# Blank TensorE steps planned up to a share of 0.9 in place of 0.7, with a new set of order keys

## The chip, the cores and the metric

The kernel runs on one core of a Trainium2 chip. The metric is the device time of one execution in microseconds, as the median of several runs. The engines are called PE (TensorE, matrix products), DVE (VectorE), ACT (ScalarE), POOL (GpSimd) and SP (SyncE, which here only issues transfers).

## What is computed

The reference is an attention in which a query may look only at the keys of its own hash bucket, followed by a two-layer feed-forward block:

```python
q_bits = (einsum('bhsd,dk->bhsk', q, proj) > 0)        # 4 batches, 8 heads, 768 rows, 64 wide, 6 bits
mask   = q_bucket[:, :, :, None] == k_bucket[:, :, None, :]
scores = where(mask, scale * q @ k.T, -1e9)
attn   = exp(scores - max) ; attn = attn / (sum + 1e-9)
x      = (attn @ v)                                     # gathered to 3072 rows of 512
h      = x @ w_in                                       # 512 -> 2048
g      = 0.5 * h * (1 + erf(h / sqrt(2)))
out    = g @ w_out                                      # 2048 -> 512
```

## The kernel before

All of the work is written down as steps (`Step`, made by `plan.add`), each with the engine or engines that can do it, a cost per engine, what it needs, the ring of buffers that it takes a slot of, and a key. `Plan.order` then plays the steps through on a model of the engines: whenever an engine is free in the model, it takes the step with the lowest key among those that are ready there. The result is one fixed list, and the program is emitted in that list's order, so that each engine has its instructions in one order that doesn't change at run time. The keys, and for steps that several engines can do a preference per engine, come from the table `PAR`.

**Attention.** A unit is 128 queries of one head against all 768 keys. For batch 0 the first eight heads of the first pass (256 queries, 16 units) and then the second pass (512 queries) run, for the other batches all 768 queries in one pass; 192 units in all. The eight heads of the first pass, five of which are used again in the second, work with float32 scores (36 units): `head_plain` loads a head (L911), moves the keys to the lower partitions (L454 or L450 `K<-Q`), projects it onto the hash vectors on PE (L926, four products), takes signs on ACT (L932) and writes mask rows from the signs on whatever engine is free. There is one buffer for the signs, so the projection of a head waits until the masks of the head before are written. In a unit PE makes the scores (L976 in float32; L978 and L979 in float16 later), DVE their maximum (L982), ACT the exponentials (L996). Then, in batch 0, PE turns the exponentials round through PSUM (L1051, copied out by ACT or DVE as `pt`) and multiplies them by the values in float32 (L1128); in the other batches they are split into a high half (any of three engines) and a low half (DVE, L1011), SP issues a transposing transfer (L1018), and PE multiplies by the values in float16 (L1137). Scores have two PSUM buffers (`s`), everything else of PE shares four (`hp`).

**Weights.** w_in and w_out arrive in 32 transfers, DVE decodes each with three instructions (L742, L747, L752), PE makes sums of squares (L765), and each block is split into a high and a low float16 half.

**Feed-forward.** For each of 12 pieces of 256 rows there are two groups; each has 8 blocks of 12 products with w_in (L1367), their evacuation by ACT (L1377), a gelu by ACT (L1405), a split into halves (high half L450/L454, low half on DVE at L1419), and 8 blocks of 6 products with w_out (L1449). The last product group of a piece is drained by DVE (L1479) and stored. Whatever of this isn't done when the last attention unit ends is left for PE at the end.

**Blank steps.** `add_blank` (L404 to L412) adds 128 optional steps, each with four products of a zero 128x128 tile with itself (L409) into a slot of `hp`. They have the key 5000, behind all others, so the planner puts one in only where PE has nothing else that is ready in the model. It also puts none in where the share of recent time in which the model's PE was active is above `FILL` (0.7): the variable `full` in `order`. A step carries a weight `act` for that share (0.6 for float32 scores, 0.5 for float32 projections, 1 for most), so a PE that does only float32 scores without a pause doesn't count as fully active. Steps that the plan didn't reach when all else was placed are left out. Once in the list a blank step is an instruction like any other: PE runs it at its place, whether or not PE would have had a pause there.

Of the kernel before, what the change touches and what calls it, by code (L numbers as in the profile page):

```python
# [34 lines left out]
GROW = ("p","hl")  # L35

PAR = dict(
    KM=91.05, KM_ACT=-197.05, KM_DVE=73.07, KM_Pool=12.06, RN=-144.89, RT=-17.08, RC_ACT=-242.77, RC_DVE=-47.89,
    XH_ACT=4.7, XH_DVE=-82.19, XH_Pool=87.66, XL_DVE=89.94, XL_Pool=357.43, VB=-258.79, GU_DVE=128.11,
    GU_Pool=-25.12, SH_DVE=118.63, SH_ACT=328.9, SH_Pool=79.99, SF_DVE=143.39, SF_ACT=-210.56, SF_Pool=-126.49,  # L40
    SU=-27.59, NM_DVE=371.98, NM_ACT=81.69, NM_Pool=10.86, NM_SP=-49.3, NL_DVE=-98.16, NL_Pool=534.95, NK_DVE=206,
    NK_ACT=268.55, NK_Pool=141.99, Z=140.46, VS0=156.74, H0=141.06, HL=-168.99, VS=-5.57, G2=140.72, HQ=274.94,
    VQ=-118.77, in0=-452.28, out0=234.8, in1=178.74, out1=35.31, in2=-733.22, out2=42.81, in3=-257.05, out3=-39.12,
    H1=85.11, H2=-180.28, H3=-76.25, H4=-254.49, H5=599.36, H6=267.16, H7=-91.77, MEV=211.52, MGE=10.33, MSP=148.58,
    V0=130.06, QK0=757.86, QK1=394.91, QK2=-27.6, MX0=5.05, MX1=-340.43, MX2=-112.33, EX0=-363.39, EX1=-245.52,
    EX2=174.69, NR0=190.13, NR1=-108.68, NR2=-84.17, HI0=-114.82, HI1=-178.05, HI2=438.46, LO0=-267.63, LO1=-47.95,
    LO2=-1120.34, PV0=-759.1, PV1=34.43, PV2=-112.01, TR0=102.85, TR1=-188.58, TR2=162.62, V1=405.09, V2=-110.24,
    Sin0=389.65, Sin1=4.89, Sin2=-162.86, Sin3=184.08, Sout0=112.78, Sout1=-94.3, Sout2=-76.09, Sout3=124.51,
    Lin=297.95, Pin=102.99, Qin=672.15, Cin=28.97, Min=-82.56, Lout=25.44, Pout=-325.05, Qout=524.38, Cout=-497.62,
    Mout=109.33, G0=17.44, G1=-32.16, G3=-43.19, G4=148.57, G5=171.52, G6=-434.49, G7=115.01, DUP0=113.75,  # L50
    DUP1=88.45, DUP2=1354.21, LOW0=225.26, LOW1=166.21, LOW2=29.11, PRJ0=120.95, PRJ1=279.7, PRJ2=-425.18,
    MSK0=-273.6, MSK1=129.08, MSK2=-126.48, DI_ACT=4.6, DI_DVE=81.25, DI_Pool=367.94, WS_ACT=-138.04, WS_DVE=-169.9,
    WS_Pool=156.82, WH_ACT=60.55, WH_DVE=42.49, WH_Pool=-4.63, WL_ACT=-275.05, WL_DVE=200.58, WL_Pool=-447.71,
    VH_ACT=500.86, VH_DVE=-763.86, VH_Pool=-164.87, RND_ACT=178.09, RND_DVE=126.86, RND_Pool=168.39, HI_ACT=65.35,
    HI_DVE=-0.25, HI_Pool=-348.7, EV_ACT=-270.89, EV_DVE=-778.22, EV_Pool=-113.05, GH_ACT=-94.28, GH_DVE=72.85,
    GH_Pool=-34.78, NS0=-43.2, NS1=520.91, NS2=-67.43,
)
FULL = 65504.0
BIG = 2.0**34
# [18 lines left out]
class Plan:  # L78
# [17 lines left out]
    QUEUE = 2.0  # L96
    PORT = 0.1
    WINDOW = 3.413
    FILL = 0.7
    FALLS = 0.45  # L100

    def __init__(self, rings):
# [3 lines left out]
    def add(self, engine, cost, emit, key, needs=(), takes=None, table=None, port=False, act=1.0, spare=False):  # L106
        s = Step(len(self.steps), engine, cost, emit, key, needs, takes, table, port, act, spare)
        self.steps.append(s)
        return s
# [12 lines left out]
    def order(self):  # L122
# [34 lines left out]
        while events and count < total:  # L157
# [25 lines left out]
            for engine, pool in ready.items():  # L183
# [3 lines left out]
                if engine == "PE":  # L187
                    w = int(now / self.WINDOW)
                    share = busy.get(w, 0.0) / self.WINDOW
                    share += busy.get(w - 1, 0.0) / self.WINDOW * (w + 1 - now / self.WINDOW)  # L190
                    full = share > self.FILL
                for s in pool:
# [75 lines left out]
def tile_bucket_attention_moe(  # L268
# [193 lines left out]
    def affine_on(name, n, pointer=False, cuts=0.0):  # L462

        more = 0.11 if name == "RND" else 0.0
        return {
            e: (affine_cost(e, n, pointer) + more + cuts * (e == "Pool"), PAR[f"{name}_{e}"])
            for e in ("ACT", "DVE", "Pool")
        }
# [35 lines left out]
    def set_up():  # L504
# [36 lines left out]

        key = PAR["SU"]
        a = add("Pool", 1.4, sums, key, [])
# [63 lines left out]
    def head(b, h, i, key, clear, cl):  # L607
# [90 lines left out]
        for half in range(2):  # L698
            for k, dst in enumerate((0, 1)):
                box = []  # L700

                def mask(half=half, k=k, dst=dst, box=box):
# [6 lines left out]
                on = {  # L709
                    "DVE": (0.18, PAR["NK_DVE"]), "ACT": (0.53, PAR["NK_ACT"]), "Pool": (0.56, PAR["NK_Pool"])  # L710
                }
# [160 lines left out]
    def values_whole(b, pr, key):  # L872
        def load():
            nc.sync.dma_start(out=whole_of(raw, pr), in_=v[b, :, words(pr)].rearrange("(c p) d -> p c d", p=P))

        raw = add("SP", 1.43, load, key - PAR["VQ"], takes="vhl")
        return raw, raw
# [6 lines left out]
    def values_halves(b, pr, key, scaled):  # L884
# [13 lines left out]

        raw = add("SP", 1.43, load, key - PAR["VQ"], takes="vraw")
        hi = add(affine_on("VH", S, True), 0, high, key, [raw, scaled], takes="vhl", port=True)  # L900
# [4 lines left out]
    def head_plain(b, h, i, key, clear, cl):  # L905
# [10 lines left out]
        loaded = add("SP", 0.85, load, key - PAR["HQ"], clear)  # L916
        mv = add(affine_on("KM", S), 0, move, key + PAR["KM"], [loaded], port=True)
        space = add("none", 0, lambda: None, key, [loaded], takes="sign")
# [20 lines left out]
        for half in range(2):  # L939
            for k, x in enumerate(both_of):  # L940
                box = []

                def mask(half=half, k=k, x=x, box=box):
# [6 lines left out]
                on = {  # L950
                    "DVE": (0.27, PAR["NK_DVE"]), "ACT": (0.53, PAR["NK_ACT"]), "Pool": (0.56, PAR["NK_Pool"])
                }
# [588 lines left out]
```

## Time and profile before

| | us |
|---|---|
| median of 3 runs | 893.41 (890.1 to 893.73) |
| the profiled execution | 894.34 |
| its span, first to last instruction | 892.5 |
| PE busy | 862.8 (97%) |
| DVE busy | 668.4 (75%) |
| ACT busy | 616.0 (69%) |
| POOL busy | 445.8 (50%) |
| blank products on PE (220) | 18.2 |
| start of the last attention score product | 708.97 |

The busy share is a mean over three stages: the start (loads, weights, float32 attention), a middle in which attention and feed-forward run side by side, and an end from 709 us in which only feed-forward is left. The columns of a stretch by engine say more than the mean.

### The profile page before, as it was taken

Reading aid. Unit: us, or ns where it says so; the run is one execution under the profiler, and the core shown is the slowest. Engines: PE = TensorE matmul, PEld = TensorE weight load, DVE = VectorE, ACT = ScalarE, POOL = GpSimd, SP = SyncE. Lnnn points to the kernel's source line nnn. Section 1 sums busy time; section 2 is a strip of 40 time slices with the busy share of each in tenths; the row PEclk is TensorE's granted clock in tenths of the full one; section 3 lists DMA queues with packets and bytes.
Section 4 is the critical chain, followed back from the end, with each engine's and each line's share of the span. In section 5 each row is a group of like instructions: output and inputs, shape, how many; then the busy total and the mean of one; then the engine's idle time right before and its main releaser. Section 6 shows DMA issues by size and latency. Waiting matters only on the chain. (4 is left out here: it accounts for less than half of the span.)

```text
span 892.5 us, 18301 instructions
## 1 busy us (share of the span) xinstructions
PE 862.8 (97%) x6953; PEld 577.6 (65%) x6953; DVE 668.4 (75%) x1356; ACT 616.0 (69%) x1058; POOL 445.8 (50%) x560
## 2 busy tenths in 40 slices
PE   7999999999999999999999999999999999999998
PEld 4566666676667757656657657667657667576663
DVE  5999798998899898988889889878897841212122
ACT  4767868799898778896979887897864823232221
POOL 2437948487666658666756675674752500000000
PEclk9999999999999999999999999999999999999999
DMA  9753261415789899797788988868787540000000
GB/s 311 238 175 105 76 182 38 145 46 107 168 168 172 160 219 186 133 170 160 133 154 198 166 154 151 146 126 146 134 136 125 113 95 1 24 1 24 1 25 24
DMA packets 282424, 112.34 MB, mean 126 GB/s; under 512 B 228704, under 2 KB 269920, under 8 KB 282336
## 3 DMA queue, kind: packets, MB, share of 16 engines
q1 hardware_dynamic: 282032, 111.18, 58.6%
q8 instruction: 54, 0.88, 0.4%
q14 instruction: 34, 0.28, 0.1%
q10 hardware_dynamic: 304, 0.00, 0.0%
HBM read 43.13 MB, written 6.29 MB: 55 GB/s over the span
## 5 line engine op out<-in xcount | busy, mean ns | idle before, releaser
L1367 PE MATMUL hp<-x,Win 128*128 128x256 f16 x2304 | 265.9, 272 | 0.3 <-DVE x L1162 0.2
L1449 PE MATMUL hp<-Wout,g 128*128 128x512 f16 x1152 | 262.6, 379 | 0.0
L1367 PEld LDWEIGHTS <-Win 128*128 128x128 f16 x2304 | 224.1, 98 | 37.5 <-issue 2.4
L1449 PEld LDWEIGHTS <-g 128*128 128x128 f16 x1152 | 110.9, 98 | 124.5 <-issue 2.8
L982 DVE TENSOR_REDUCE rows<-s 128x1 f32<-128x768 f32 x192 | 180.1, 947 | 8.9 <-PE s L976 4.0
L996 ACT ACTIVATE p<-s,rows 128x768 f32<-128x768 f32 x143 | 141.3, 989 | 12.1 <-POOL rows L454 3.8
L1377 ACT ACTIVATE h<-hp,ffs 128x512 f32<-128x512 f32 x96 | 65.5, 683 | 99.6 <-PE hp L1367 99.1
L978 PE MATMUL s<-Q 88*128 88x384 f16 x304 | 99.5, 327 | 7.3 <-ACT p L996 4.1
L979 PE MATMUL s<-K 128*128 128x384 f16 x304 | 99.2, 326 | 0.0
L454 DVE TENSOR_SCALAR g<-h,ffs 128x512 f16<-128x512 f32 x28 | 14.2, 509 | 110.6 <-ACT h L1405 79.4
L987 POOL TENSOR_SCALAR rows<-rows,hs 128x1 f32<-128x1 f32 x84 | 58.9, 702 | 44.0 <-DVE rows L982 39.4
L1137 PE MATMUL hp<-pt,vhl 128*64 128x256 f16 x1296 | 77.2, 274 | 2.6 <-DMA pt<-wraw 1.0
L1011 DVE SCALAR_TENSOR_TENSOR hl<-p,rows,hl 128x768 f16<-128x768 f32 x68 | 70.8, 1043 | 11.5 <-POOL hl L454 8.1
L1419 DVE SCALAR_TENSOR_TENSOR g<-h,ffs,g 128x512 f16<-128x512 f32 x96 | 75.7, 801 | 3.9 <-POOL g L454 1.1
L1137 PEld LDWEIGHTS <-vhl 128*64 128x64 f16 x1296 | 69.2, 110 | 12.5 <-issue 10.7
L476 POOL TENSOR_TENSOR K<-raw,Q 64x768 f16<-64x768 f32 x37 | 63.6, 1718 | 3.1
L454 POOL TENSOR_SCALAR rows<-rows 128x1 f32<-128x1 f32 x95 | 38.3, 403 | 36.2 <-ACT p L996 16.9
L996 ACT ACTIVATE wraw<-s,rows 128x768 f32<-128x768 f32 x49 | 48.4, 987 | 9.9 <-POOL rows L454 6.8
L979 PEld LDWEIGHTS <-K 128*128 128x128 f16 x304 | 29.8, 98 | 28.5 <-issue 12.6
L454 POOL TENSOR_SCALAR raw<-raw,hs 64x768 f32<-64x768 f32 x39 | 43.8, 1122 | 5.4 <-ACT Q L450 1.9
L978 PEld LDWEIGHTS <-Q 88*128 88x128 f16 x304 | 29.7, 98 | 25.8 <-issue 8.5
L1405 ACT ACTIVATE h<-h 128x2048 f32<-128x2048 f32 x24 | 45.9, 1911 | 0.4
(176 smaller groups left out, 1322.4 us busy)
## 6 DMA issues: line engine op xcount, KB each, us to landing
raw<-qk SPq DMA_DIRECT2D x27, 384.0 KB, 3.9
vraw<-v SPq DMA_DIRECT2D x24, 384.0 KB, 4.0
wraw<-w_in SPq DMA_DIRECT2D x16, 512.0 KB, 5.3
wraw<-w_out SPq DMA_DIRECT2D x16, 512.0 KB, 3.9
out<-o SPq DMA_DIRECT2D x11, 512.0 KB, 3.1
K<-Q SPq DMA_DIRECT2D x32, 96.0 KB, 2.3
Q<-qk SPq DMA_DIRECT2D x6, 384.0 KB, 8.0
Q<-Q SPq DMA_DIRECT2D x19, 96.0 KB, 2.3
```

The lines of the kernel that those rows point to most:

```text
L454: on.tensor_scalar(out=o, in0=x, scalar1=scale, scalar2=bias, op0=ALU.mult, op1=ALU.add)
L476: on.tensor_tensor(out=o, in0=x, in1=y, op=ALU.subtract)
L978: nc.tensor.matmul(to, aq[kk, qs], ak[kk, n], start=True, stop=False)
L979: nc.tensor.matmul(to, bq[:, qs], bk[:, n], start=False, stop=True)
L982: nc.vector.tensor_reduce(out=nm, in_=both(sp), axis=AX.XY, op=ALU.max, negate=True)
L996: nc.scalar.activation(out=buf(ex).rearrange("p (b k) -> p b k", b=2), in_=both(sp), func=AF.Exp, scale=sc, bias=nb, accum_out=ssum,)
L1011: nc.vector.scalar_tensor_tensor(out=buf(hi)[:, 1], in0=buf(ex), scalar=r, in1=buf(hi)[:, 0], op0=ALU.mult, op1=ALU.subtract,)
L1137: nc.tensor.matmul(pv[j * D : (j + 1) * D], buf(vh)[:, tv, kt, j * D : (j + 1) * D], buf(holds[j][0])[:, tp * KT + kt, :nt], start=kt == 0 ...
L1367: nc.tensor.matmul(buf(pair[0])[:, j * ch[1] : (j + 1) * ch[1]], win_hl[:, f0 // WB1, tw, pr, f0 % WB1 : f0 % WB1 + P], x[:, tx, pr, : ch[1]],
L1377: nc.scalar.activation(out=values_of()[:, 2 * fp : 2 * fp + 2, :nt], in_=buf(pair[0])[:, : 2 * nt].rearrange("p (j k) -> p j k", j=2), fun ...
L1419: nc.vector.scalar_tensor_tensor(out=gt[:, 1, s2, :nt], in0=h[:, s2, :nt], scalar=sg, in1=gt[:, 0, s2, :nt], op0=ALU.mult, op1=ALU.subtract,)
L1449: nc.tensor.matmul(buf(banks[u]).rearrange("p (c f) -> p c f", c=NWB), gt[:, tg, f, u * P : (u + 1) * P], wout_hl[:, :, tw, ft], start=ft ...
```

## The change

One number of the planner and all of the numbers of `PAR` differ; no other line does.

```diff
 PAR = dict(
-    KM=91.05, KM_ACT=-197.05, KM_DVE=73.07, KM_Pool=12.06, RN=-144.89, RT=-17.08, RC_ACT=-242.77, RC_DVE=-47.89,
+    KM=338.56, KM_ACT=93.78, KM_DVE=-125.94, KM_Pool=-40.06, RN=20.65, RT=-108.24, RC_ACT=-170.72, RC_DVE=19.05,
...
-    FILL = 0.7
+    FILL = 0.9
```

The steps are the same, except for the number of blank products: 220 before, 244 now. What differs is where each step stands, and which engine does the steps that several can do.

The first place is on PE near the start, at the third score unit. In the names `Q_90` and `K_91` are a head's queries and keys, `p` the exponentials, `hash` the hash vectors, `diag` and `sums` small tiles, and the numbers are buffers. Before, from the scores of that unit on:

```order
L976 MATMUL s_61<-K_91,Q_90 128x384 x2
L976 MATMUL s_62<-K_91,Q_90 128x384 x2
L1051 MATMUL hp_63<-ident_131,p_67 128x128 x3
L1051 MATMUL hp_64<-ident_131,p_67 128x128 x3
L1051 MATMUL hp_65<-ident_131,p_68 128x128 x3
L1051 MATMUL hp_66<-ident_131,p_68 128x128 x3
L926 MATMUL hp_63<-Q_116,hash_140 32x384 x4
L409 LDWEIGHTS blank
L409 MATMUL hp_64<-blank 128x128
```

Now, at the same unit:

```order
L976 MATMUL s_61<-K_91,Q_90 128x384 x2
L1051 MATMUL hp_65<-ident_131,p_67 128x128 x3
L1051 MATMUL hp_63<-ident_131,p_67 128x128 x3
L926 MATMUL hp_66<-Q_94,hash_140 32x384 x4
L976 MATMUL s_62<-K_91,Q_90 128x384 x2
L491 LDWEIGHTS ones
L491 MATMUL hp_65<-diag_87,ones 128x128
L1051 MATMUL hp_63<-ident_131,p_68 128x128 x3
L1051 MATMUL hp_66<-ident_131,p_68 128x128 x3
L926 MATMUL hp_65<-Q_116,hash_140 32x384 x4
L976 MATMUL s_61<-K_93,Q_92 128x384 x2
L976 MATMUL s_62<-K_93,Q_92 128x384 x2
```

Before, 12 blank products follow this piece, and 80 stand between the third and the 22nd unit; now none stands there. Ahead of the third unit there are now 148 in place of 112: 24, 24, 40, 32 and 28 in a row, where there were 24, 16, 4, 32, 8 and 28.

The second place is on SP at its very start. Before, the loads of weights (`wraw<-w_in`) stand between those of the heads (`<-qk`):

```order
L911 DMA x_110<-qk 128x768
L735 DMA wraw_82<-w_in 128x2x512
L735 DMA wraw_83<-w_in 128x2x512
L911 DMA Q_114<-qk 128x768
L911 DMA Q_88<-qk 128x768
L617 DMA raw_77<-qk 128x768
L735 DMA wraw_84<-w_in 128x2x512
L911 DMA Q_90<-qk 128x768
```

Now five heads come first, and `Q_88`, of which the first scores are made, is third; its projection on PE is the third one in both orders:

```order
L911 DMA Q_114<-qk 128x768
L911 DMA Q_90<-qk 128x768
L911 DMA Q_88<-qk 128x768
L911 DMA x_110<-qk 128x768
L911 DMA Q_92<-qk 128x768
L735 DMA wraw_82<-w_in 128x2x512
L735 DMA wraw_83<-w_in 128x2x512
L735 DMA wraw_84<-w_in 128x2x512
```

The third place is on PE late in the second pass, after the last projection of a head and before the first products with w_out. Before, 20 blank products stand in a row there, behind the projection (L685):

```order
L685 MATMUL hp_66<-K_95,hash_136 32x384
L409 LDWEIGHTS blank
L409 MATMUL hp_63<-blank 128x128
...
L1051 MATMUL hp_64<-ident_131,p_67 128x128 x3
L1051 MATMUL hp_63<-ident_131,p_67 128x128 x3
L978 LDWEIGHTS Q_92
L978 MATMUL s_62<-Q_92 128x384
```

Now 28 stand ahead of the two small products L577 (which serve a head's scale) and 32 behind them, and then come scores:

```order
L409 MATMUL hp_64<-blank 128x128
L577 LDWEIGHTS twin
L577 MATMUL hp_65<-tops,twin 128x1
...
L409 LDWEIGHTS blank
L409 MATMUL hp_63<-blank 128x128
...
L978 LDWEIGHTS Q_90
L978 MATMUL s_62<-Q_90 128x384
```

Between the 22nd unit and the first product with w_out there are 88 blank products (28 before), and ahead of that first product stand 192 products with w_in (168 before) and 19 float16 units (18 before). Behind the last score of all, 696 products with w_in, 432 with w_out and 108 with values remain (720, 438 and 108 before). Eight blank products now stand after the very last product.

## Rows read from the trace of the kernel before

**Rows 1.** The page's busy times: microseconds, share of the span and instructions of each engine.

```profile
PE 862.8 (97%) x6953; PEld 577.6 (65%) x6953; DVE 668.4 (75%) x1356; ACT 616.0 (69%) x1058; POOL 445.8 (50%) x560
```

**Rows 2.** Busy time of each engine by stretch (from:to, length, then PE, weight loads, DVE, ACT, POOL with instructions in brackets, the granted clock of PE, the share of the DMA engines, GB/s).

```profile
0.00:26.50 26.50, 19.87 (x182) 12.25 (x182) 16.36 (x43) 13.83 (x21) 7.55 (x25) 1.00 0.93 319
26.50:100.00 73.50, 68.65 (x502) 44.48 (x499) 67.75 (x144) 51.76 (x100) 42.77 (x68) 1.00 0.49 152
100.00:209.70 109.70, 104.99 (x923) 76.39 (x921) 97.84 (x230) 89.64 (x170) 73.32 (x107) 1.00 0.33 92
209.70:709.10 499.40, 489.62 (x4090) 325.72 (x4089) 440.65 (x868) 410.36 (x707) 318.27 (x357) 1.00 0.83 156
709.10:892.50 183.40, 179.68 (x1268) 118.79 (x1265) 45.75 (x74) 50.36 (x62) 3.94 (x5) 1.00 0.09 25
200.00:250.00 50.00, 49.43 (x389) 32.95 (x388) 43.59 (x83) 45.11 (x80) 34.79 (x39) 1.00 0.72 137
200.00:425.00 225.00, 219.80 (x1826) 145.44 (x1825) 201.29 (x398) 188.91 (x336) 153.22 (x168) 1.00 0.84 163
```

**Rows 3.** PE in order of time up to the third score unit: start, duration, engine, line, tiles, shapes, count, and in brackets the idle time before it and who ended it.

```profile
0.98 2.74 PE L409 MATMUL hp<-blank 128*128 128x128 bf16 x24 [0.98 <-DVE hash L392]
6.58 1.50 PE L926 MATMUL hp<-x,hash 64*32 64x384 f32 x8 [2.87 <-DVE hash L399]
9.85 0.59 PE L409 MATMUL hp<-blank 128*128 128x128 bf16 x4
11.09 1.44 PE L409 MATMUL hp<-blank 128*128 128x128 bf16 x12 [0.65 <-DVE both_offs L535]
12.46 1.51 PE L926 MATMUL hp<-Q,hash 64*32 64x384 f32 x8
15.68 1.50 PE L926 MATMUL hp<-Q,hash 64*32 64x384 f32 x8
17.76 1.72 PE L409 MATMUL hp<-blank 128*128 128x128 bf16 x28 [0.25 <-DVE hs L580]
19.61 2.82 PE L976 MATMUL s<-K,Q 76*128 76x384 f32 x8
22.36 0.85 PE L926 MATMUL hp<-Q,hash 64*32 64x384 f32 x8
23.59 0.62 PE L765 MATMUL hp<-Win 128*128 128x128 bf16 x8
26.49 2.85 PE L976 MATMUL s<-K,Q 76*128 76x384 f32 x8
```

**Rows 4.** PE in order of time between the third score unit and the last: the two largest pauses of the float32 stretch, the blank product behind the 22nd unit, the 20 blank products in a row and what follows them, the first products with w_out, and the last product of the last score.

```profile
34.82 0.85 PE L926 MATMUL hp<-Q,hash 64*32 64x384 f32 x8 [0.90 <-DVE pt L454]
46.06 1.56 PE L976 MATMUL s<-K,Q 76*128 76x384 f32 x4 [0.97 <-ACT p L996]
...
99.98 0.39 PE L409 MATMUL hp<-blank 128*128 128x128 bf16 x4
...
191.40 1.29 PE L409 MATMUL hp<-blank 128*128 128x128 bf16 x20
193.49 0.88 PE L1051 MATMUL hp<-ident,p 128*128 128x128 f32 x6 [0.80 <-ACT p L996]
...
209.74 1.46 PE L1449 MATMUL hp<-Wout,g 128*128 128x512 f16 x6
...
708.97 0.33 PE L979 MATMUL s<-K 128*128 128x384 f16 x1
```

**Rows 5.** The costliest groups, DVE: line, engine, operation, tiles and shapes, count, then busy microseconds, mean nanoseconds of one, and idle time before them with who ended it.

```profile
L982 DVE TENSOR_REDUCE rows<-s 128x1 f32<-128x768 f32 x192 | 180.1, 947 | 8.9 <-PE s L976 4.0 <-PE s L979 3.6 <-POOL Wout L476 0.3
L651 DVE SCALAR_TENSOR_TENSOR K<-raw,hs,Q 64x768 f16<-64x768 f32 x15 | 18.4, 1225 | 0.4
L454 DVE TENSOR_SCALAR pt<-hp 128x384 f32<-128x384 f32 x34 | 18.2, 547 | 0.9 <-PE hp L1051 0.7 <-PE hp L1128 0.2
L454 DVE TENSOR_SCALAR o<-Wout,tiny 128x1024 f32<-128x1024 f32 x1 | 0.7, 742 | 0.0
```

**Rows 6.** The same view for ACT.

```profile
L450 ACT ACTIVATE hl<-p,rows 128x768 f16<-128x768 f32 x32 | 29.8, 931 | 17.7 <-DMA pt<-hl 8.8 <-DVE rows L987 3.8 <-DVE rows L1005 2.7
L450 ACT ACTIVATE Q<-Q 64x768 f16<-64x768 f16 x7 | 5.9, 842 | 0.1
```

**Rows 7.** Three pieces of the chain that ended last (start, duration, engine, tile, line, count): products with w_in, with w_out and with values, in a stretch where PE doesn't pause.

```profile
584.81 3.93 PE hp L1367 x36
579.59 2.59 PE hp L1449 x12
588.74 2.09 PE hp L1137 x36
```

**Rows 8.** Waits of PE: its tile and line, whom it waited for, microseconds in total, times, longest.

```profile
PE s L978 <- ACT p L996: 4.1, 9, 1.1
PE s L978 <- ACT wraw L996: 2.7, 4, 1.2
PE hp L1137 <- DMA pt<-wraw: 1.0, 2, 0.8
```

**Rows 9.** The end of the run, all engines in order of time.

```profile
884.36 5.53 SPq L1492 DMA_DIRECT2D out<-o  x2
888.82 0.69 DVE L1479 TENSOR_TENSOR o<-hp,ffs 128x512 f32<-128x512 f32 x1 [4.49 <-PE hp L1449]
```

More of the change, by code (lines that the diff above doesn't have):

```diff
@@ L37 @@
 PAR = dict(
-    KM=91.05, KM_ACT=-197.05, KM_DVE=73.07, KM_Pool=12.06, RN=-144.89, RT=-17.08, RC_ACT=-242.77, RC_DVE=-47.89,
[L39 to L56, printed above, removed]
+    KM=338.56, KM_ACT=93.78, KM_DVE=-125.94, KM_Pool=-40.06, RN=20.65, RT=-108.24, RC_ACT=-170.72, RC_DVE=19.05,
@@ new lines @@
+    XH_ACT=210.16, XH_DVE=7.74, XH_Pool=90.78, XL_DVE=-38.28, XL_Pool=158.1, VB=-151.09, GU_DVE=-336.98,
+    GU_Pool=82.95, SH_DVE=-5.82, SH_ACT=-334.92, SH_Pool=-49.18, SF_DVE=21.85, SF_ACT=-104.94, SF_Pool=195.36,
+    SU=-83.27, NM_DVE=86, NM_ACT=-377.53, NM_Pool=-30.66, NM_SP=96.75, NL_DVE=-136.18, NL_Pool=196.74,
+    NK_DVE=-120.63, NK_ACT=-102.29, NK_Pool=10.06, Z=128.09, VS0=-88.2, H0=-48.93, HL=-59.64, VS=129.22, G2=3.26,
+    HQ=295.77, VQ=110.09, in0=79.2, out0=106.24, in1=141.19, out1=168.42, in2=136.87, out2=-115.55, in3=3.35,
@@ new lines @@
+    out3=68.94, H1=191.2, H2=-99.08, H3=-118.34, H4=-332.48, H5=-80.76, H6=254.37, H7=-127.62, MEV=276.73,
+    MGE=-178.16, MSP=66.8, V0=-72.8, QK0=-93.51, QK1=-108.37, QK2=108.6, MX0=-450, MX1=-150.62, MX2=115.85,
+    EX0=-64.03, EX1=137.4, EX2=25.14, NR0=-8.44, NR1=-67.14, NR2=1035.93, HI0=78.66, HI1=110.34, HI2=154.08,
+    LO0=102.73, LO1=-341.19, LO2=-125.71, PV0=190.15, PV1=69.77, PV2=62.11, TR0=227.29, TR1=61.09, TR2=92.8,
+    V1=-72.28, V2=-97.32, Sin0=-126.57, Sin1=-110.63, Sin2=-73.46, Sin3=233.87, Sout0=-26.39, Sout1=-410.31,
@@ new lines @@
+    Sout2=-240.13, Sout3=-125.09, Lin=254.46, Pin=800.99, Qin=-200.36, Cin=121.44, Min=208.69, Lout=-586.01,
+    Pout=-56.05, Qout=-674.79, Cout=322.69, Mout=105.44, G0=-90.72, G1=43.02, G3=94.77, G4=-158.67, G5=-135.69,
+    G6=471.19, G7=52.78, DUP0=-52.55, DUP1=146.67, DUP2=382.24, LOW0=196.35, LOW1=-139.71, LOW2=61.45, PRJ0=158.56,
+    PRJ1=-57.69, PRJ2=85.39, MSK0=129.53, MSK1=30.9, MSK2=-29.16, DI_ACT=-204.87, DI_DVE=-62.27, DI_Pool=-86.29,
+    WS_ACT=-98.19, WS_DVE=-8.9, WS_Pool=-0.46, WH_ACT=133.09, WH_DVE=-86.05, WH_Pool=77.47, WL_ACT=140.41,
@@ L57 @@
+    WL_DVE=123.78, WL_Pool=92.94, VH_ACT=288.88, VH_DVE=110.93, VH_Pool=54.59, RND_ACT=153.06, RND_DVE=-61.11,
+    RND_Pool=-75.2, HI_ACT=-187.83, HI_DVE=119.13, HI_Pool=-61.07, EV_ACT=-109.55, EV_DVE=178.44, EV_Pool=-39.2,
+    GH_ACT=-77.39, GH_DVE=20.88, GH_Pool=170.2, NS0=38.42, NS1=6.74, NS2=221.4,
 )
```

## The prediction

> **What bounds the kernel now.** I read the busy times first, then the same by stretch, then each engine in order of time, and last the waits. PE is busy 862.8 of 892.5 us, far above DVE with 668.4 [rows 1], and the stretches say where the rest is [rows 2]. From 709.1 us PE is alone: 179.68 busy of 183.40, and what is missing there is the last drain and store [rows 9]. From 209.7 to 709.1 it pauses for 499.40 - 489.62 = 9.8 us, mostly until exponentials have freed a score buffer [rows 8]. Before 209.7 it pauses for 6.6, 4.9 and 4.7 us in the three stretches, and there also run the 220 blank products: the kernel's slack lies at the start. With PE's work fixed, the time is that work, plus the blanks, plus the pauses, so a new order can give back at most some 45 us, and each change of order is worth what it does to blanks and pauses.
>
> The start is bound differently from the rest. Between 26.5 and 100 us DVE is busy 67.75 of 73.50 us, nearly as long as PE with 68.65, which includes the blanks [rows 2]. PE pauses there for a copy by DVE or for exponentials [rows 4], and both engines have to be fed for that stretch to shorten.
>
> **The price of a blank.** 24 in a row took 2.74 us at 0.98 us, 0.114 each; 28 in a row took 1.72 us at 17.76, 0.061 each [rows 3]. The projections show the same step: 1.50 at 6.58, 12.46 and 15.68 us, 0.85 at 22.36. So PE runs at its lower level (1.2 GHz) up to about 17 us and at the upper (2.4 GHz) from there, though the clock column reads 1.00 in all stretches [rows 2]. A blank in a real pause costs nothing; one ahead of work that was ready costs its time.
>
> **Part by part, in order of time.** FILL decides only how many blanks stand in the list; nearly all else that moves is moved by the keys.
>
> (a) *Up to the third score unit: +1.0 us.* 36 more blanks stand there. Before, the second projection starts at 12.46, the third at 15.68, the first score at 19.61, the third unit at 26.49 [rows 3]. Now 20 blanks follow from 11.09 (a slot had to come free there) at 0.114: 13.4. The projection takes 1.5: 14.9. Of the next 40 blanks some 20 run slowly, until 17.1, and 20 at 0.061: 18.3. There the third projection starts, 2.6 us late. From it to the first score were 19.61 - 15.68 = 3.9 us, for signs and masks; less the 0.65 that the projection takes less at full clock, the first score comes at 21.6 if the 32 blanks (2.0 us) fit between. Then two units (1.4 each), two projections (0.8 each) and 28 blanks (1.7) stand ahead of the third unit, which comes at about 27.8, 1.3 late. One projection more and one set of squares (0.6) fewer are done by then, which leaves +1.0. The bounds are 0 (DVE, which has other work there, decides) and +2.4. The loads of five heads ahead of the weights bring the scores no earlier, since the buffer for signs lets one head through at a time.
>
> (b) *Third to 22nd unit: -3.0 us.* PE's work there is the same but for one set of squares; 80 blanks are gone, 80 x 0.061 = 4.9 us, beside 4.9 us of pauses. Were PE the only bound, this would give nearly 9.8. But DVE has the same 67.75 us of work there and only 73.50 - 67.75 = 5.8 us to spare [rows 2], so 5.8 is the most. I take half of it, as DVE has to wait for others here and there too. Bounds -5.8 and 0: the pauses can stay where the blanks were.
>
> (c) *22nd unit to the first product with w_out: +1.0 us.* 60 more blanks stand here, 60 x 0.061 = 3.7 us. Before, the 20 in a row took 1.29 us and the exponentials came another 0.80 later [rows 4], so at least there PE really had nothing to do. On the other side DVE gets less to do before its first low half of g: three score maxima (0.947 each) and five copies of pt (0.547) fewer, three 128x1024 pieces of weights (0.742) fewer; three low halves of heads (1.225) and two subtractions of 128x1024 weights more [rows 5]. The trace has none of those on DVE; by the maximum over 768 and by the 768-wide low halves it is 0.9 to 1.7, and I take 1.3. That makes -2.8 - 2.7 - 2.2 + 3.7 + 2.6 = -1.4 us, and small steps as much again. So from all extra blanks (+3.7) to a gain of 1.0: I take +1.0. 24 products with w_in and a score unit are done here that stood later; that moves work, and PE's total stays.
>
> (d) *The middle: 0.* At the last score 24 products with w_in (36 took 3.93 us, so 2.6) and 6 with w_out (12 took 2.59, so 1.3) less are left for the end [rows 7]: 3.9 us less behind that point. It is a gain only if the last score comes at the same time, so if the 3.9 us fit into PE's 9.8 us of pauses; if PE has no more pauses than it had, the last score comes 3.9 later and nothing changes. Added steps: ACT gets nine more high halves of exponentials (0.931) and five more copies (0.842) over the run [rows 6], and small ones, some 14 us in all; POOL gets 29 us less, DVE about 4 more. ACT has 499.4 - 410.4 = 89 us to spare and DVE 59 [rows 2]. I take 0, between -4 and +6.
>
> (e) *The end: 0.* The eight last blanks start when the last product is through, beside the drain (0.69) and the store, which end the run at 892.5 [rows 9].
>
> Sum: +1.0 - 3.0 + 1.0 = -1.0 us on the profiled 894.34, that is 893.3. The median before is 893.41, 0.9 lower, so I predict 892.4.
>
> **A rule against the change.** From 17 us on, PE shows the upper level in all rows, with pauses up to 0.97 us among them [rows 4]. More blanks have no clock to win there, and fewer could lose one. The Trainium skill ("TensorE: Matmul & The Clock Gate", Part 1, The HAM clock gate) says that the lower level is the default and comes back after an idle stretch of PE. The trace agrees for the level at the start and shows no return. By that rule the 80 blanks that go in (b) were a guard.
>
> **The rivals.**
>
> *Faster: the start packs.* In (b) DVE gets its whole 5.8 us, and in (c) the blanks fall into pauses and DVE's relief counts (-1.0). With (a) at +1.0 that is -5.8; with 1 us from the middle -6.8, so 886.6. For it: PE's order from the third to the 22nd unit has no filler left, so whatever DVE releases PE can use. Against it: DVE at 67.75 of 73.50 us is hardly ever free there. Chance 0.32.
>
> *Slower: ACT comes late in the middle.* ACT makes the exponentials on which PE already waits [rows 8]. From 200 to 425 us it is busy 188.91 of 225.00 us, and its densest 50 us are 45.11 [rows 2]. By the 112th unit the new order has given it the larger part of its 14 us more, which would bring that stretch to about 200, or 89%, close to the 90% of the densest piece. If half of the 14 can't be hidden, PE waits 7 us more: 892.4 + 7 = 899.4. It decides from 5.5 us on. For it: the waits on exponentials are the largest of PE's. Against it: part of that work comes earlier rather than in addition, and POOL, which is relieved by 29 us, also feeds the exponentials. Chance 0.18.
>
> *Slower: the clock falls in (b)*, where the scores run in float32 without fillers. At the lower level 10 us of PE's work cost 10 more, so about 902. Against it: PE has 60 us of work there in at most 73, and pauses were never over 1 us after 17 us. Chance 0.05.
>
> *The change does nothing*, since the clock was full and PE's sum is fixed: then 893.4, inside my forecast.
>
> **How the numbers follow.** About 0.5%, 4.5 us, is what a measurement of this kernel can tell from no change: 888.9 and below is faster, 897.9 and above slower. The forecast of 892.4 with the case of no effect has 0.45; faster 0.32; slower 0.18 + 0.05 = 0.23. The likeliest case alone reaches from 889 to 897. For 8 in 10 the range must take in most of the faster and of the first slower case: with (b) at -5.8, (c) at -1, (d) at -3 and (a) at +1 the time is 884.6; with (d) at +6 and (c) at +3 it is 900.4, and the slower cases lie at 899 and 902. I give 884 to 901.
>
> **What would show it.** (a): third score unit at 27 to 28 us in place of 26.49. (b): what follows the 22nd unit comes at 97 to 99 us in place of 99.98 [rows 4], DVE over 93% busy between. (c): the 60 blanks run without a pause behind them if they cost, and with one if they were free; the first product with w_out between 209 and 213 us (209.74 before [rows 4]). (d): the last score at 707 to 713 us in place of 709 [rows 4], and 175.5 to 176 us from it to the end of PE's work; PE's waits on exponentials of 6 to 8 us. ACT's share above 90% between 200 and 425 us, with those waits above 12 us, would speak for the slower rival; a projection or score at double length after 17 us for the clock. I am wrong altogether if PE's pauses in the middle go far from 9.8 us, since no term above prices a shift of that order there.

## The result, and the profile after

The changed kernel takes 897.41 us (median of 6 runs, 895.13 to 899.64) beside 892.82 for the kernel before in the same comparison: a ratio of 1.0053, 95% interval 1.0038 to 1.0069. I had forecast 892.4, no change. The profiled execution is one of 898.22 us with a span of 896.4, so 3.9 more than before.

The page's busy times [rows 1]:

```profile
PE 866.5 (97%) x6977; PEld 580.7 (65%) x6977; DVE 675.8 (75%) x1364; ACT 629.8 (70%) x1081; POOL 416.5 (46%) x525
```

Busy time by stretch, cut at the marks of the prediction (third score unit, blanks behind the 22nd, first product with w_out, last score), and two pieces of the third stretch; columns as in [rows 2]:

```profile
0.00:28.35 28.35, 21.43 (x212) 14.90 (x212) 17.54 (x43) 12.36 (x20) 6.47 (x23) 1.00 0.95 326
28.35:94.35 66.00, 62.09 (x425) 39.62 (x423) 63.20 (x130) 52.07 (x110) 31.16 (x52) 1.00 0.49 154
94.35:216.60 122.25, 116.46 (x1020) 83.88 (x1018) 107.04 (x245) 100.74 (x186) 76.45 (x112) 0.97 0.35 93
216.60:716.70 500.10, 490.12 (x4085) 325.83 (x4082) 442.91 (x877) 415.10 (x708) 300.31 (x337) 1.00 0.79 153
716.70:896.40 179.70, 176.37 (x1247) 116.52 (x1244) 45.13 (x73) 49.53 (x60) 2.15 (x3) 1.00 0.10 24
100.00:125.00 25.00, 22.41 (x197) 14.21 (x197) 22.67 (x46) 15.59 (x36) 8.43 (x13) 0.93 0.68 187
125.00:150.00 25.00, 23.73 (x179) 17.21 (x181) 19.42 (x50) 21.78 (x37) 18.58 (x28) 0.93 0.23 65
```

The clock column is new: 0.97 in the third stretch, 0.93 in two of its pieces, where the kernel before has 1.00 in every row [rows 2]. The second stretch is 7.5 us shorter than before (73.49), the third 12.5 longer (109.72), the middle 0.8 longer and the end 3.8 shorter.

PE in order of time [rows 3, 4]: the start, then the places where the clock falls, the blanks near 185 us, and the marks:

```profile
11.11 2.29 PE L409 MATMUL hp<-blank 128*128 128x128 bf16 x20 [0.80 <-DVE both_offs L535]
13.33 1.50 PE L926 MATMUL hp<-Q,hash 64*32 64x384 f32 x8
18.24 0.85 PE L926 MATMUL hp<-Q,hash 64*32 64x384 f32 x8
22.15 1.56 PE L976 MATMUL s<-K,Q 76*128 76x384 f32 x4
28.35 1.51 PE L976 MATMUL s<-K,Q 76*128 76x384 f32 x4
...
94.35 1.72 PE L409 MATMUL hp<-blank 128*128 128x128 bf16 x28
...
101.30 1.56 PE L976 MATMUL s<-K,Q 76*128 76x384 f32 x4
105.23 1.44 PE L1051 MATMUL hp<-ident,p 128*128 128x128 f32 x6 [2.37 <-DVE hl L454]
106.59 3.72 PE L1128 MATMUL hp<-pt,vhl 128*64 128x256 f32 x20
...
129.53 1.82 PE L1367 MATMUL hp<-x,Win 128*128 128x256 f16 x9 [0.78 <-DVE hs L580]
...
185.25 0.61 PE L409 MATMUL hp<-blank 128*128 128x128 bf16 x8
186.57 1.28 PE L409 MATMUL hp<-blank 128*128 128x128 bf16 x20 [0.72 <-DVE pt L454]
187.90 1.95 PE L409 MATMUL hp<-blank 128*128 128x128 bf16 x32
...
216.62 1.47 PE L1449 MATMUL hp<-Wout,g 128*128 128x512 f16 x6
...
716.73 0.33 PE L979 MATMUL s<-K 128*128 128x384 f16 x1
```

Behind the scores at 101.30 PE waits 2.37 us for a copy by DVE. What follows runs at the lower level (1.2 GHz): 20 products of L1128 take 3.72 us; 24 take 2.81 at the upper level (experiments below). Six products of L1051 take 1.44 us where they took 0.82 at 99.24. A second such piece follows at 129.53, where 9 products with w_in take 1.82 us (12 take 1.47 in e1, last section); PE's pauses just before it are 0.78 us at most.

DVE just there, in order of time, and POOL beside it:

```profile
100.74 0.89 DVE L742 TENSOR_SCALAR Wout<-wraw 128x512 int32<-128x512 int32 x1 [0.97 <-DMA wraw<-w_out]
101.55 2.12 DVE L752 SCALAR_TENSOR_TENSOR Wout<-wraw,Wout 128x512 int32<-128x512 int32 x1
103.70 1.01 DVE L651 SCALAR_TENSOR_TENSOR K<-raw,hs,Q 64x768 f16<-64x768 f32 x1
104.75 0.42 DVE L454 TENSOR_SCALAR hl<-hp 128x256 f32<-128x256 f32 x1
...
101.43 1.69 POOL L476 TENSOR_TENSOR K<-raw,Q 64x768 f16<-64x768 f32 x1
```

The copy of hl, which frees PE's slot, stands in DVE's order behind two steps of decoding w_out. DVE waits 0.97 us for their transfer, and the second takes 2.12 us in place of the usual 0.68.

PE's waits for exponentials [rows 8] are no longer than they were:

```profile
PE s L978 <- ACT p L996: 4.6, 13, 0.8
PE hp L1051 <- DVE hl L454: 2.4, 1, 2.4
PE s L978 <- ACT wraw L996: 0.8, 2, 0.6
```

### The profile page after: what moved, and what is told of

It reads as the page before. It is cut to its first block, busy times and chain, and to the rows that moved or that the text cites. A ratio compares the mean times of both kernels' runs of the same rounds, so it can differ in the third digit from the quotient of the medians.

```text
span 896.4 us, 18331 instructions
## 1 busy us (share of the span) xinstructions
PE 866.5 (97%) x6977; PEld 580.7 (65%) x6977; DVE 675.8 (75%) x1364; ACT 629.8 (70%) x1081; POOL 416.5 (46%) x525
## 5 line engine op out<-in xcount | busy, mean ns | idle before, releaser
L996 ACT ACTIVATE p<-s,rows 128x768 f32<-128x768 f32 x140 | 138.0, 987 | 29.4 <-POOL rows L454 21.2
L978 PE MATMUL s<-Q 88*128 88x384 f16 x304 | 99.3, 327 | 6.4 <-ACT p L996 4.6
L454 DVE TENSOR_SCALAR g<-h,ffs 128x512 f16<-128x512 f32 x34 | 17.9, 529 | 108.4 <-ACT h L1405 77.8
L987 POOL TENSOR_SCALAR rows<-rows,hs 128x1 f32<-128x1 f32 x68 | 50.7, 746 | 63.1 <-DVE rows L982 43.4
L476 POOL TENSOR_TENSOR K<-raw,Q 64x768 f16<-64x768 f32 x38 | 66.2, 1741 | 3.2
L996 ACT ACTIVATE wraw<-s,rows 128x768 f32<-128x768 f32 x52 | 51.3, 986 | 10.0 <-POOL rows L454 6.9
L454 POOL TENSOR_SCALAR hl<-p,rows 128x768 f16<-128x768 f32 x32 | 34.8, 1089 | 40.4 <-DMA pt<-hl 28.1
```

Of the source, the lines that this page charges most:

```text
L454: on.tensor_scalar(out=o, in0=x, scalar1=scale, scalar2=bias, op0=ALU.mult, op1=ALU.add)
L476: on.tensor_tensor(out=o, in0=x, in1=y, op=ALU.subtract)
L978: nc.tensor.matmul(to, aq[kk, qs], ak[kk, n], start=True, stop=False)
L996: nc.scalar.activation(out=buf(ex).rearrange("p (b k) -> p b k", b=2), in_=both(sp), func=AF.Exp, scale=sc, bias=nb, accum_out=ssum,)
```

## The experiments

The theory: the loss stands between the 22nd unit and the first product with w_out; the new order makes pauses of PE there behind which the clock falls, at places where it has no blanks. The rivals: the blanks themselves cost their time; a hole near 185 us, where ACT is away for the first gelu, got longer; DVE has too much to do there. The runs go by the first part of their labels (e1 to e16), each with the median of the kernel before on the same chip in brackets where it is first told, and with its ratio to it. Runs of different chips are set beside each other by their distance from their own kernel before; for the changed kernel that is 4.6 us.

**What the blanks are worth.** Four kernels leave blanks out, by their place among the planned ones; one lets the old keys plan with 0.9. The 60 near 185 us out of the changed kernel:

```diff
         for s in steps:
+            n_blank += s.spare
+            if s.spare and 44 < n_blank <= 59:
+                continue
             s.emit()
```

> The changed kernel without the 60 blank products that stand in a row late in the second pass (185 to 190 us in its trace); every other instruction in the same order. If the order is what costs (PE has nothing to run there, because ACT is loading tables and making the first gelu and so makes no exponentials), the blanks are free and the time stays at the 897.4 us of the changed kernel within 1 us, or rises by about 1.7 us if the clock now falls in the hole. If the blanks cost their own time, it falls by 60 x 0.061 = 3.7 us to 893.7.

897.05 us [893.42], 1.0043 (1.0027 to 1.0059): no gain. The scores behind that place start 5.38 us after the last product ahead of it without the blanks (180.99 to 186.37) and 5.39 us after it with them (184.42 to 189.81), so the 3.7 us that I had charged for them were not on the path. In its profile the clock falls in that hole instead. All 96 behind the third unit out (`n_blank > 37`):

> The changed kernel without all 96 blank products behind the third score unit (28 at 94 us, 60 at 185 us, 8 at the end). If the order costs: 897 to 901 us, with one or two falls of the clock more than the two of the changed kernel, about 1.7 us each. If the blanks cost: 88 x 0.061 = 5.4 us less, 892.0.

896.71 us, 1.0051 (1.0030 to 1.0072): nothing either; the clock is at the lower level from 104.6 us for 3.4 us and from 186.5 for 6.8. The same in the kernel before (`n_blank > 28`, 108 out):

> The kernel before without its 108 blank products behind the third score unit, order otherwise the same. If those blanks hold the clock up, the clock falls here once to three times between 30 and 210 us, where the kernel before has no fall, and the time rises by about 1.7 us a fall to 894.5 to 898. If the blanks cost their own time and hold nothing, 108 x 0.061 = 6.6 us less, 886. If they are free and hold nothing, 892.8.

899.72 us, 1.0077 (1.0058 to 1.0096). Busy time by stretch in that run, second stretch and two of its pieces:

```profile
26.49:99.98 73.49, 64.85 (x385) 39.53 (x382) 63.37 (x132) 47.03 (x91) 36.24 (x58) 0.88 0.44 140
50.00:75.00 25.00, 22.42 (x127) 14.74 (x128) 21.55 (x48) 13.39 (x30) 6.95 (x13) 0.86 0.60 188
75.00:100.00 25.00, 24.88 (x137) 14.65 (x136) 19.80 (x40) 15.82 (x29) 16.03 (x24) 0.80 0.20 59
```

PE in order of time there, where the clock first falls:

```profile
50.07 2.14 PE L976 MATMUL s<-K,Q 76*128 76x384 f32 x4 [2.03 <-ACT p L996]
```

The blanks of the kernel before hold its clock up, and are worth some 6 us. Without them the old order loses its clock in the stretch in which the new order keeps it without any. The two falls there begin behind PE's longest pauses of that stretch, 2.03 us here and 1.53 us ahead of the scores at 74.52; the longest pause that the new order has there is 0.87 us. The 72 blanks in rows of 40 and 32 ahead of the first scores, out of the changed kernel (`12 < n_blank <= 30`):

> The changed kernel without the 72 blank products in rows of 40 and 32 ahead of its first scores. If they delay the start, as step (a) has it, the third projection comes up to 1.5 us earlier, the third score unit 1 to 2 us earlier, and the time falls by about 1 us to 896.4, or less if the clock now rises later. If DVE decides there, it stays at 897.4.

898.38 us [892.26], 1.0068 (1.0046 to 1.0091). PE in order of time, the first and the third unit:

```profile
19.70 2.93 PE L976 MATMUL s<-K,Q 76*128 76x384 f32 x4
...
29.78 1.94 PE L976 MATMUL s<-K,Q 76*128 76x384 f32 x4
```

The scores start earlier than at 22.15, but at the lower level (2.93 against 1.56), and the third unit comes later than at 28.35: nothing is gained without these blanks. And the old keys with `FILL = 0.9`:

> The old keys with the new limit of 0.9 alone: the planner now puts in all 512 blank products, among them 76 in a stretch before the first product with w_out and 80 in a stretch in the middle, and its order moves everywhere. If blanks cost their own time: 292 x 0.061 = 17.8 us more, 911. If only the holes cost that the blanks stand in: two holes of some 4.8 us where the kernel before has one of 2.1, so 898 to 902. If the limit alone were what made the changed kernel slower by 4.6 us, about 897.

909.69 us [893.42], 1.0186 (1.0163 to 1.0210): 0.9 alone, without the new keys, loses 16 us, close to the first case of what was expected, in which blanks cost their own time. In the profile PE is busy 879.3 us in place of 862.8 and pauses in all about as long as before (30.3 us, 29.7 before). Most of the added work is the 292 added blanks (512 take 36.2 us of PE, 220 took 18.2), a part is the clock, which is at the lower level for some 10 us near 205 us. The order moves everywhere as well, so this run doesn't part the limit from the order that it makes. With 0.7 the planner leaves steps of the new keys without a place, so there is no such kernel to run.

**The pauses.** 60 blanks by hand in the changed kernel, 32 ahead of the L1051 of the pause near 103 us, 8 and 20 near 128 us:

```diff
+        places, n_pe = {105: (8, 0), 132: (2, 1), 134: (5, 0)}, 0
         for s in steps:
+            if s.engine == "PE" and not s.spare:
+                count, slot = places.get(n_pe, (0, 0))
+                for _ in range(4 * count):
+                    nc.tensor.matmul(bufs["hp"][slot][:, :P], blank, blank, start=True, stop=True)
+                n_pe += 1
             s.emit()
```

> The changed kernel with 60 blank products more, put by hand where its trace has pauses of PE just before the granted clock falls: 32 where PE waits 2.37 us at 102.9 us, 8 and 20 around its pauses at 127.7 to 128.5 us. If the falls of the clock are a part of the loss, the clock stays at the upper level between 94 and 216 us and the time falls by 2 to 3.4 us, to 894.0 to 895.4. If the loss lies in the order alone, it stays at 897.4. If blanks cost their own time, it rises by 60 x 0.061 = 3.7 to 901.

894.30 us [892.26], 1.0022 (1.0009 to 1.0036): 2.0 us above its kernel before where the changed kernel stands 4.6 above, so 2.6 better, with 60 blanks more. Its profile has a clock of 1.00 at both places. Next, without blanks, DVE's two decoding steps behind the copy of hl:

```diff
+        late = [steps[552], steps[554]]
+        steps[563:563] = late
+        del steps[554], steps[552]
         for s in steps:
```

> The changed kernel with two steps of DVE later in its order: the L742 that decodes a block of w_out and the L752 behind it (at 100.7 and 101.6 us in the profile of the changed kernel, where DVE first stood 0.97 us for the transfer of that block and the L752 then took 2.12 us) now stand behind the copy of hl (L454) for which PE paused 2.37 us. Everything is still done. Theory 'a pause in the new order lets the clock fall': the pause at 102.9 us goes or shrinks below 1 us, no stretch at the lower level follows near 105 us, so at most the one near 130 us is left, and the first product with w_out comes 2 to 4 us earlier: 894 to 896 us beside 897.4. Rival 'the clock falls by itself, wherever': the time stays at 897.4 within 1 us and the fall comes at another place.

895.54 us [892.29], 1.0043 (1.0027 to 1.0059), at the upper end of what was expected, and its interval doesn't part it from 897.4. Its profile has a clock of 1.00 in all of these pieces, though the pause only shrank from 2.37 to 1.90 us, not below 1. That is the one execution of ten with a mean granted clock of 1.000; the others show 0.992 to 0.998, so they had falls somewhere, whether here or, as e15's profile (0.996) shows them, in the first 15 us. Both edits together:

> The changed kernel with the blank products ahead of the pauses near 103 and 128 us and with the two steps of decoding of w_out behind the copy of hl on DVE; the split of g stays where the changed kernel has it, and everything is still done. It tells what these two mends give together. Theory 'both act by keeping the clock up, so they don't add': 893.5 to 895, like the blanks alone (894.3). Rival 'the two are separate losses': 3.1 + 1.9 = 5.0 us less than 897.4, so 892.4.

892.91 us [892.95], 0.9989 (0.9977 to 1.0002): the whole loss is gone. PE in order of time in the three kernels, e5, e9 and e15, from the scores ahead of the pause (e5's stand at 100.95):

```profile
102.34 1.95 PE L1509 MATMUL hp<-blank 128*128 128x128 bf16 x32
104.88 1.15 PE L1051 MATMUL hp<-ident,p 128*128 128x128 f32 x6 [0.58 <-DVE hl L454]
```

```profile
100.36 1.56 PE L976 MATMUL s<-K,Q 76*128 76x384 f32 x4
101.75 0.49 PE L1051 MATMUL hp<-ident,p 128*128 128x128 f32 x3
104.15 0.55 PE L1051 MATMUL hp<-ident,p 128*128 128x128 f32 x3 [1.90 <-DVE tiny L787]
104.62 2.81 PE L1128 MATMUL hp<-pt,vhl 128*64 128x256 f32 x24
```

```profile
100.74 1.56 PE L976 MATMUL s<-K,Q 76*128 76x384 f32 x4
102.14 1.95 PE L1512 MATMUL hp<-blank 128*128 128x128 bf16 x32
103.92 1.15 PE L1051 MATMUL hp<-ident,p 128*128 128x128 f32 x6
105.00 2.81 PE L1128 MATMUL hp<-pt,vhl 128*64 128x256 f32 x24
```

From those scores to the first L1128 it is 106.59 - 101.30 = 5.29 us in the changed kernel, 5.00 in e1, where the clock stays up past this pause (rows in the last section), and 4.26 in e9 and e15. So DVE's order at this place costs 0.7 us by itself. The falls of the clock can be read in two ways. Beside e1, in which the same pauses stand at both places and the clock stays up, the changed kernel takes 1.6 us more at each: 10.62 us in place of 9.00 from the scores at 101.30 to the next, and 3.53 in place of 1.96 from the products at 129.53 to the next scores. And e5, which differs by the guards alone, needs 2.65 us less from the blanks behind the 22nd unit to the first product with w_out (119.62 beside 122.27, table below): part of the 3.2 is spent on other waits, such as 0.61 us for exponentials ahead of the scores at 121.31. With the 0.7 that makes 3.4 of the 3.9 us by which the profiled execution is longer.

By the ratios the two edits are worth 0.0031 and 0.0010 alone and 0.0064 together; by the medians beside their own kernels before it is 2.6 and 1.3 us alone and 4.6 together. That e15 stands 2.1 us lower than e5 in this way is not to be seen in their profiled executions, which differ by 0.2 us (893.46 and 893.70): e15 is 0.8 ahead at the first product with w_out, counted from the third unit, and loses that again in the middle. Where the rest comes from stays open.

| | third unit | behind 22nd | first w_out | last score | span |
|---|---|---|---|---|---|
| before | 26.49 | 99.98 | 209.74 | 708.97 | 892.5 |
| changed | 28.35 | 94.35 | 216.62 | 716.73 | 896.4 |
| e5 | 27.47 | 94.00 | 213.62 | 712.00 | 891.7 |
| e9 | 26.93 | 93.41 | 212.75 | 713.14 | 892.8 |
| e15 | 27.62 | 93.80 | 213.01 | 712.24 | 891.9 |

**The hole near 185 us.** The first gelu as an exponential in the changed kernel, which takes out two table loads; then the same in the kernel before:

```diff
-            nc.scalar.activation(out=h, in_=h, func=AF.Gelu)
+            nc.scalar.activation(out=h, in_=h, func=AF.Gelu if n else AF.Exp)
```

> The changed kernel with the first of its 24 gelus computed as an exponential (this changes the values of the first group of the first piece): the two table loads of 1.28 us around it go, the order stays. If PE's hole at 185 to 190 us comes from ACT being away from the exponentials for 4.5 us, it shrinks by about 2.6 us and the time falls to 894.8. If PE is held there by something else, or the time is regained later anyway, it stays at 897.4.

> The same edit in the kernel before, whose hole behind the first gelu is 2.1 us (191.4 to 193.5). If that hole has the same cause, it goes and the time falls by 1.3 to 2.1 us, from 893.4 to 891.3 to 892.1. If not, it stays at 893.4.

897.59 us, 1.0061 (1.0038 to 1.0083), so no gain, and 891.23, 0.9990 (0.9977 to 1.0004) [892.26], which is not to be told from no change. In the changed kernel the 60 blanks stand in PE's way by then: it goes from them into the scores without a pause (187.90 + 1.95 is 189.85, and the scores start at 189.81). So both out, on top of the blanks by hand of e5, first without the 60 alone:

> The changed kernel with the 60 blank products placed by hand ahead of its pauses near 103 and 128 us (as in the earlier experiment that gave 894.3) and without the planned 60 in the hole near 185 us. Everything is still done. Theory 'blanks are free in a hole and a guard elsewhere': without the 60 the hole stays, with the clock perhaps falling in it, so 894 to 896. Theory 'the 60 cost their time': 3.7 us less, 890 to 891.

896.21 us [892.29], 1.0058 (1.0035 to 1.0080), so 1.9 more than e5. PE in order of time there:

```profile
182.88 0.19 PE L577 MATMUL hp<-tops,twin 128*128 128x1 bf16 x2 [2.20 <-DVE tops L620]
185.25 0.48 PE L978 MATMUL s<-Q 88*128 88x384 f16 x1 [2.18 <-ACT p L996]
185.52 0.53 PE L979 MATMUL s<-K 128*128 128x384 f16 x1
```

The pause is as long as the blanks were, and the scores behind it take 0.53 us in place of 0.33. The planned 60 are a guard here. And with the gelu as an exponential as well:

> The kernel of the run before with the first gelu of the first piece computed as an exponential, which changes the values of that group and takes away ACT's two table loads of 1.28 us around it. If the hole near 185 us is ACT being away for the gelu (its two loads and 1.9 us of work), then with neither the blanks nor the loads in the way the scores start some 2.6 us earlier: 891.5 to 893. If the hole has another end (DVE's copies, the order of PE), the time is that of the run before within 1 us.

897.11 us, 1.0060 (1.0038 to 1.0081): no gain, where 891.5 to 893 was the theory. The scores do come earlier behind the last product before them, but then PE pauses 2.81 us on a chain that goes back to DVE's maximum, which stands behind DVE's split of g.

**DVE's place of the split of g.** Its five steps as one block behind the maxima of the next units, first on e11, then on e10, then with both edits of e15 and the planned 60:

```diff
+        late_g = [steps[i] for i in (1021, 1028, 1040, 1043, 1056)]
+        steps[1108:1108] = late_g
+        for i in (1056, 1043, 1040, 1028, 1021):
+            del steps[i]
```

> The kernel of the earlier run with hand-placed blanks, without the planned 60 and with the first gelu computed as an exponential (its values change), and in addition DVE's five steps of the first group's split (one high half of g, four low halves at L1419, some 3.9 us of work) stand later in DVE's order, behind the maxima and pt copies of the next four units; nothing waits for them for another 20 us. Theory 'in the hole near 185 us DVE is what is late once ACT is not': the second pause of PE there (2.81 us, behind a chain from DVE's maximum) goes or falls below 1.2 us, and the first product with w_out comes 1.5 to 3 us earlier against its third unit than in that run: 894 to 896 beside 897.1. Rival 'the order of PE decides': the pauses stay at 5 to 6 us in all, and so does the time within 1 us.

> The same move of DVE's five steps with the gelu as it is; everything is still done. Theory 'ACT and DVE are both late there': the scores are still held until ACT is back, some 5 us behind the last product, so the first part of the hole stays and only what comes behind it shrinks: within 1 us of the 896.2 of the run without the move. If DVE alone set the hole: 893 to 894.

> The changed kernel with all three mends at once: blank products ahead of the pauses near 103 and 128 us, the two steps of decoding of w_out behind the copy of hl on DVE, and DVE's split of g later; the planned 60 blanks are kept and everything is still done. Theory 'the loss stands between the 22nd unit and the first product with w_out, in the falls of the clock and in pauses that a place in DVE's order makes': 891 to 893.5, so the whole loss of 4.6 us is gone or nearly so. Rival 'the new order has more work for DVE in that stretch and pays for it anywhere': 894 to 896, as with the blanks alone.

897.81, 901.55 and 898.27 us [892.76]; 1.0060 (1.0044 to 1.0076), 1.0102 (1.0084 to 1.0119) and 1.0067 (1.0051 to 1.0083), all three above what the theory gave. The pause that I aimed at is gone, and a new one stands 10 us later. DVE and PE in order of time in e13:

```profile
197.94 4.38 DVE L1419 SCALAR_TENSOR_TENSOR g<-h,ffs,g 128x512 f16<-128x512 f32 x4
202.25 0.32 DVE L987 TENSOR_SCALAR rows<-rows,hs 128x1 f32<-128x1 f32 x2
...
203.87 0.48 PE L978 MATMUL s<-Q 88*128 88x384 f16 x1 [2.87 <-ACT wraw L996]
204.14 0.52 PE L979 MATMUL s<-K 128*128 128x384 f16 x1
```

My block held up the small steps L987 that ACT's next exponentials need; PE waits 2.87 us, and the clock falls again. In e14, beside e15 only this block is more, and the ratio goes from 0.9989 to 1.0067. Last, the five steps one by one behind the L987:

```diff
+        g_split = [(1021, 1115), (1028, 1115), (1040, 1122), (1043, 1143), (1056, 1158)]
+        moved = {b: [steps[a] for a, at in g_split if at == b] for _, b in g_split}
+        gone = {a for a, _ in g_split}
+        steps = [s for i, t in enumerate(steps) for s in ([] if i in gone else [t]) + moved.get(i, [])]
```

> The same, with DVE's split of g later but not in one block: the high half and the first low half behind DVE's steps that release the exponentials of the next units (L987), the other three low halves singly behind later steps. In the run where all five stood in one block ahead of L987, a pause of 2.83 us of PE came of it. Theory 'DVE's order decides': no pause of PE over 1.5 us between 188 and 205 us, and the first product with w_out comes 2 to 4 us earlier against the third unit than in that run (216.90 - 27.31 = 189.6), so 185.6 to 187.6, and the time is 892 to 894. Rival: a pause of 2 us or more stays there, and the time is 896 or more.

894.41 us [892.95], 1.0019 (1.0010 to 1.0029): the pause is gone (none over 0.92 us from 188 to 205 us) and the first product with w_out comes 185.8 us behind the third unit, as expected, but e15 has 185.4 without any move, and the time is 1.5 above e15. So the split stood well where the changed kernel has it, and the theory that it makes the hole falls. The hole stays; the loss is explained without it, by e15.

## Why the prediction was right or wrong

*(a) +1.0, right.* The profiled execution says +1.9 (28.35). The third unit of the 13 profiled kernels that have this start unchanged lies between 26.06 and 28.35, middle one 27.31, against 25.89, 26.49 and 26.54 for the three of the old start: +0.8. One profile settles this mark only to about 1 us.

*(b) -3.0, undersized: -7.5.* My bound of 5.8 us rested on DVE having the same work there. It has 63.20 us now and had 67.74: the new order pushes 4.5 us of it behind the mark. DVE's share is 96% of the shorter stretch, as I had said it would be over 93%.

*(c) +1.0, between -1.0 and +3.7: the step that failed.* The stretch is 12.5 us longer. Of that 3.9 is work that only moved here (24 products with w_in 2.6, a score unit 0.7, a set of squares 0.6), so the step measured +8.6. Three things stood in it that I had not priced, and above all I had put the clock at nothing here. First, I counted DVE's relief up to its first low half of g, a mark which the new order itself brings forward (from 197.36 to 188.42 us); over the whole stretch DVE has not less but 9.2 us more (107.04 against 97.86), of which 4.5 are what left (b). Second, a place in DVE's order that makes PE wait 2.37 us, which costs 0.7. Third, the two falls of the clock, 1.6 us each. The 60 blanks, which I charged with 3.7 us, were not on the path (e1).

With the two edits of e15 the same step is 119.21 - 109.76 - 3.9 = +5.5, and (b) is -7.3: together -1.8, where I had -2.0. And 892.91 us for e15 is where I had put the changed kernel (892.4). That agreement is in part luck: (b) and (c) are each some 4.5 us off and cancel, since DVE's work moved from the one to the other, which I had not foreseen. In the sum, what I missed is the falls of the clock and the 0.7 us of DVE's order. That those two account for the loss is shown by e5 and e15 and by the rows of e1; e9 alone is not to be told from the changed kernel. That the second slips in because the transfer of w_out and POOL's L476 come just then is read from the trace only.

*(d) and (e) 0, right.* The middle is 0.8 us longer and the end 3.8 shorter, the 3.9 of moved work that I had counted. PE's waits for exponentials on L978, of which [rows 8] has 6.8 us, are 5.4 now (4.6 and 0.8), below my 6 to 8; with those on L976 it is 7.1 in place of 8.1.

*The rivals.* "The start packs": its half in (b) came, and more (-7.5); its half in (c) did not. "ACT comes late": not borne out, by those waits. "The clock falls in (b)": right in kind, wrong in place and price. (b) kept its clock without a single blank; the falls came in (c), where the blanks also lie but not at the pauses, and cost some 3 us in place of 10. The rule that I set against the change held in e3, where the old order without its blanks lost 6 us. My sentence that more blanks have no clock to win there is refuted by e5.

## What to carry to other kernels

Look in a new order for the places where a copy that frees PE stands on its engine behind a step that waits for a transfer: the pause is paid once as idle time and may be paid again by the clock behind it. A relief counted "up to" an instruction says nothing if the change moves that instruction; count over stretches with the same work in both orders, and look in the next stretch for what left the last. Price filler by the pause that it covers, not by the piece: 60 pieces cost nothing in one hole and gave 2.6 us at two others, and in e4, whose order moved as well, 292 more cost 16.

## What the runs showed of the hardware

The same pause doesn't always cost the clock. PE in order of time in e1, behind the pause near 103 us and at the next place where the changed kernel loses its clock; the two kernels have the same order up to there:

```profile
104.50 1.14 PE L1051 MATMUL hp<-ident,p 128*128 128x128 f32 x6 [2.37 <-DVE hl L454]
105.57 2.81 PE L1128 MATMUL hp<-pt,vhl 128*64 128x256 f32 x23
...
127.76 1.47 PE L1367 MATMUL hp<-x,Win 128*128 128x256 f16 x12 [0.78 <-DVE hs L580]
```

Both paused 2.37 us and later 0.78. e1 goes on at the upper level (23 products in 2.81 us, 12 in 1.47), the changed kernel at the lower (20 in 3.72, 9 in 1.82; rows of the first section). Nor does the length of a pause alone decide in these traces: in e2 a pause of 1.38 us near 95 us did not lower the clock, and in e14 one of 2.83 us near 203 us did not either, while one of 2.87 us at the same place in e13 did. So an order that pauses is a risk that is paid in some executions, and one profile shows one draw.

DVE's L752 takes 2.12 us in place of 0.68 where it starts 0.11 to 0.12 us behind POOL's L476 of 1.69 us, as in the rows of the changed kernel above; it ends 0.55 us behind POOL's instruction (103.67 and 103.12), as if it began its work when POOL was through. In e8, where the transfer comes later, the L742 ahead of it meets the L476 in its stead, and takes 1.75 us in place of 0.42, and the L752 takes 0.68. The Trainium skill ("SBUF — State Buffer", SBUF: two separate sides) says that DVE and GpSimd share a pair of ports that one of them holds for a whole instruction, so that the other waits until it is through; for DVE this holds where it has two inputs in SBUF, against a GpSimd instruction that reads SBUF, or runs in a mode that uses two ports. The traces agree for the L752, which has two inputs (2.12 us). The L742 has one, and no run shows in which mode it ran. No run took the L476 away either.
